# An attention and mixture-of-experts kernel: constants in one transfer, some normalisations on ScalarE, and a new order of all steps

## The chip, the cores and the metric

The kernel runs on one core of a Trainium2 chip. The metric is the device time of one execution in microseconds (us), over several executions. Matrix products run on TensorE (PE in the profile; its weight loads are shown as PEld), the other work on VectorE (DVE), ScalarE (ACT) and GpSimd (POOL); SyncE (SP) issues nearly all DMAs.

## The reference

There are 8 batches, 8 heads, 576 positions and a head width of 64. Head by head and batch by batch an attention is computed whose scores get a bias that depends on the two positions:

```python
scores = q @ k.T / 8
x      = log1p(|i - j|) / log1p(max(i, 1))        # 576 x 576
bias   = relu(x * w1 + b1) @ w2                   # hidden width 32, one bias per head
attn   = softmax(scores + bias);  y = attn @ v
```

The result, as 4608 tokens of width 512, goes through a soft mixture of experts: `logits = y @ phi` (32 slots, four per expert); a softmax over the tokens makes the inputs of the slots, each expert applies two weight matrices (512 x 1024, relu, 1024 x 512), and a softmax over the slots spreads the outputs over the tokens.

## The kernel before

**Units and tiles.** A head pair of one batch is a unit. The first head pair is cut in two halves of the rows (units 0 to 7 and 8 to 15, two tiles of 128 rows each, and half a fifth tile), the other three pairs are units 16 to 39 with four tiles and half a fifth. A tile `p` of unit `u` goes through these steps, and each has a short name:

- `S`: scores of both heads of the pair on PE, into two pairs of PSUM banks (line 517, or line 523 where the tile is done in four quarters; that is what a `+` means here).
- `t`: DVE adds the bias to the scores of one head and finds the row's extreme (line 534). `e`: ACT takes the exponential and the row sum (line 542). `a` and `m`: a small addition (line 549, on POOL, or on DVE with a `+`) and the reciprocal on DVE (line 553).
- `n`: the normalisation, a multiplication of the tile's 576 columns by one number per row, on POOL (lines 436 and 561).
- `T` and `R`: PE transposes the normalised tile into PSUM (line 495); `c` and `cR`: ACT or DVE (`+`) copy that to SBUF (line 439).
- `M0` to `M2`: the product with v on PE (line 629), `x`: its copy to SBUF, `xs`: its store.

**The bias tables.** Before and between the first units, 36 jobs make the bias: `f` (four features of a job, DVE at line 977, or ACT at line 975 with a `+`), `B` (PE, line 987), `E` (ACT at line 997, or DVE with a `+`), `D` (SP writes the result to DRAM, line 1006). `b0` to `b4` read a chunk of 128 rows of it back for a head pair (line 425); chunk 3, for example, needs the jobs 24 to 31.

**The end.** When the last head pair of a batch is done, the steps of the mixture follow (`fx`, `K`, `KR`, `L`, `D`, `d`, `W`, `C`, `Z`; `dq` contains a memset of a small tile on POOL, line 780, for which the transposes of `C` wait). Behind the last unit come the experts (`F`, `H`, `U`, `V`, `s`) and the output (`o`, `p`, `P`). `w` and `r` fetch the 64 tiles of expert weights of 512 KB.

**What sets the order.** Every step is registered with its name, and the string `ORDER` lists all 2644 of them. An entry is `name/unit`, a `+` where there is a choice of the engine (or of the form of `S`), and after `@` the PSUM banks. The program is written out in this order, so each engine and SP's queue get their instructions in the order in which the string has them; every engine works through its own in order. All bulk transfers but one go through SP, and SP, too, waits in order: a transfer that must wait for a buffer or for a write to land holds back all behind it.

**The first transfers.** `tabs` is loaded by ACT's queue, `cols` (w1, b1, w2) and `cons` (a table of reciprocals, and `rowm`) by SP, lines 336 to 338. DVE computes from them `scl` (line 341), which every `f` needs, `nb1` (line 356) and four parts of `wbd` (line 361).

Of the kernel before, what the change touches and what calls it, by code (L numbers as in the profile page):

```python
# [24 lines left out]
wm/-1 f13.2/-1+ f13.0/-1+ f14.2/-1 f9.1/-1 f13.3/-1+ f15.3/-1+ f15.0/-1 f15.1/-1+ f13.1/-1 f14.0/-1 B13/-1@0  # L25
f9.0/-1+ f15.2/-1 f12.0/-1+ f9.3/-1 B15/-1@2 f8.2/-1+ E15/-1 f9.2/-1 B9/-1@4 E9/-1 f11.1/-1+ f14.1/-1
f11.0/-1 f14.3/-1 B14/-1@6 E14/-1 f10.2/-1 f10.3/-1+ f12.1/-1 f12.2/-1 f12.3/-1 B12/-1@2 E12/-1 f11.2/-1
f11.3/-1 f10.1/-1 B11/-1@4 E11/-1 D9/-1 f10.0/-1 B10/-1@6 f23.0/-1+ f8.0/-1 D14/-1 f8.3/-1 f8.1/-1
B8/-1@2 D15/-1 E10/-1 D12/-1 f19.1/-1 f19.3/-1+ E13/-1+ D11/-1 f16.0/-1+ D13/-1 f19.0/-1 f19.2/-1
B19/-1@4 D10/-1 E8/-1+ f21.3/-1 f21.2/-1 D8/-1 f21.1/-1+ f21.0/-1 B21/-1@0 f18.1/-1+ f18.2/-1 f16.2/-1+  # L30
f18.0/-1 f18.3/-1 B18/-1@6 E19/-1 D19/-1 E21/-1 f20.2/-1 D21/-1 f16.1/-1 f16.3/-1 B16/-1@2 b1/-1
f23.1/-1 f23.2/-1 f17.1/-1 f23.3/-1+ B23/-1@4 f17.3/-1 f17.2/-1+ E16/-1+ f20.1/-1 f17.0/-1+ D16/-1 f20.3/-1+
f22.0/-1+ f20.0/-1 B17/-1@0 B20/-1@2 f22.1/-1+ E18/-1+ D18/-1 f22.3/-1+ E17/-1 D17/-1 f3.1/-1+ f22.2/-1
B22/-1@6 E22/-1 E23/-1+ E20/-1+ f0.1/-1 f5.0/-1 f5.3/-1+ f5.2/-1+ f0.2/-1+ f5.1/-1 D23/-1 f0.0/-1+
f0.3/-1 D20/-1 S1/0@0,4 t1.1/0 t1.0/0 e1.0/0 e1.1/0 S1/1+@2,6 t1.1/1 t1.0/1 D22/-1 b2/-1
f3.3/-1 B5/-1@4 f1.0/-1+ f1.1/-1 E5/-1 B0/-1@0 E0/-1 S2/0@6,2 e1.1/1 lq/2 f1.3/-1 e1.0/1
a1/0 m1/0 f1.2/-1 B1/-1@4 f3.0/-1 f3.2/-1 E1/-1 f4.3/-1 D1/-1 B3/-1@0 f2.3/-1 n1.0/0
n1.1/0 T1/0@4 E3/-1 f6.3/-1+ f2.2/-1 a1/1 D3/-1 f2.0/-1 f2.1/-1 c1/0 f4.1/-1 B2/-1@0
E2/-1 f4.0/-1 f4.2/-1 t2.1/0 e2.1/0 t2.0/0 e2.0/0 f6.1/-1+ f27.1/-1+ B4/-1@4 E4/-1+ D2/-1
a2/0+ m2/0 n2.1/0 n2.0/0 S2/1+@2,0 lq/3 m1/1 t2.0/1 e2.0/1 t2.1/1 S1/2+@6,4 t1.1/2  # L40
t1.0/2 e2.1/1 a2/1+ m2/1 T2/0@2 c2/0 f7.1/-1 S2/2@0,4 t2.1/2 t2.0/2 f24.0/-1 R2/0@6
M0/0@2 f7.3/-1 D0/-1 f25.2/-1+ cR2/0 n1.1/1 f24.1/-1+ n1.0/1 T1/1@6 c1/1 n2.1/1 n2.0/1
T2/1@4 R2/1@0 cR2/1+ e2.1/2 f7.2/-1 c2/1+ f7.0/-1 M1/0 e2.0/2 f24.2/-1+ S1/3+@6,0 t1.1/3
M2/0 f26.1/-1 f6.2/-1 x/0 xs/0 M0/1@4 a2/2 m2/2 e1.1/2 B7/-1@2 M1/1 lq/4
t1.0/3 f35.3/-1 e1.1/3 e1.0/2 a1/2+ m1/2 f27.3/-1 lv/2 S2/3+@0,6 f6.0/-1 t2.0/3 f26.0/-1+
E7/-1 M2/1 t2.1/3 D7/-1 f27.0/-1+ f27.2/-1 x/1 xs/1 e1.0/3 n2.1/2 n2.0/2 lv/3
# [1231 lines left out]
```

## Time and profile before

| | |
|---|---|
| three executions | 566.37, 567.01, 569.01 us (median 567.01) |
| the profiled execution | 566.71 us, its span 564.7 us |
| PE, PEld busy | 537.2 us (95%), 358.6 us (64%) |
| DVE, ACT, POOL busy | 430.8 us (76%), 435.8 us (77%), 232.7 us (41%) |
| DMA | 117.15 MB, mean 207 GB/s |

The profile is one execution. The busy time of an engine is the union of its instructions; PE's matmuls are pipelined and their ends are modelled, so PE can look busy where it is slowed down. Where an engine was idle before an instruction, the trace names what released it. The chain of waits is followed back from the last instruction. All times in the rows are counted from the start of the span.

### The profile page before, as it was taken

To read this page: it belongs to the slowest core of one execution; us is meant where nothing else is said; L and a number is where in the kernel's file an instruction comes from. 1 tells how busy PE (TensorE), PEld (TensorE's weight loads), DVE (VectorE), ACT (ScalarE), POOL (GpSimd) and SP (SyncE) were. 2 spreads that over 40 slices of the span, in tenths; PEclk is the share of its full clock that TensorE was granted. 3 is DMA by queue.
4 is the path that set the end of the run, shared out by engine and by line. 5 is a ranking of instruction groups with operands and counts; after the bars stand their busy time and mean duration, and the time that the engine had idled before them with its cause. 6 is when DMAs were issued, how large, how long until landed. Compare 5 with 4: busy or idle time off the path is not lost.

```text
span 564.7 us, 23724 instructions
## 1 busy us (share of the span) xinstructions
PE 537.2 (95%) x9991; PEld 358.6 (64%) x9991; DVE 430.8 (76%) x1188; ACT 435.8 (77%) x922; POOL 232.7 (41%) x365
## 2 busy tenths in 40 slices
PE   8989999999999999999999999999999899999883
PEld 5546665777786667766676666666666566753652
DVE  7999997777888878788876887887889777652241
ACT  7999997898878789887889887887877688641162
POOL 4034434464654545665464655553434354200000
PEclk9999999999999999999999999999999999989998
DMA  6854799667934334194543438455232708989988
GB/s 193 311 179 131 229 293 358 201 182 229 313 107 152 120 116 144 45 345 120 192 165 86 143 130 272 163 202 201 89 107 102 260 6 294 375 294 379 393 342 336
DMA packets 46553, 117.15 MB, mean 207 GB/s; under 512 B 5488, under 2 KB 9712, under 8 KB 46448
## 3 DMA queue, kind: packets, MB, share of 16 engines
q1 hardware_dynamic: 46304, 115.35, 59.2%
q8 instruction: 78, 1.28, 0.9%
q10 hardware_dynamic: 144, 0.29, 0.1%
q14 instruction: 27, 0.22, 0.1%
HBM read 87.01 MB, written 28.62 MB: 205 GB/s over the span
## 4 chain that ended last, share of the span: by engine, by line
PE 72%; DVE 8%; ACT 5%; DMA 3%; issue 3%; POOL 1%; SPq 1%; ACTq 0%; DVEq 0%; POOLq 0%
PE ps L629 22%; PE ps L523 17%; PE ps L495 17%; PE ps L517 5%; DVE y L534 4%; PE ps L1074 2%; ACT y L542 2%; PE ps L1147 2%; DVE f L977 2%; PE ps L709 1%; DMA out_dram<-ob 1%; PE ps L851 1%; DMA qk<-in_qk_dram 1%; DMA bias_m<-e 1%; ACT ob L439 1%
## 5 line engine op out<-in xcount | busy, mean ns | idle before, releaser
L436 POOL TENSOR_SCALAR y<-y,sm 128x576 f32<-128x576 f32 x288 | 212.8, 756 | 158.9 <-DVE sm L553 124.4
L542 ACT ACTIVATE y<-y,mn 128x576 f32<-128x576 f32 x288 | 220.6, 769 | 18.5 <-DVE mn L534 12.5
L534 DVE CUSTOM_DVE_ANT_0 y<-ps,bm 128x576 f32<-128x576 f32 x256 | 184.4, 752 | 39.6 <-PE ps L523 28.5
L629 PE MATMUL ps<-at,v 64*64 64x288 f32 (+2 forms) x2880 | 163.2, 358 | 0.6 <-issue 0.3
L523 PE MATMUL ps<-qk 64*64 64x512 f32 (+1 forms) x1840 | 139.3, 409 | 0.6 <-DVE mn L534 0.3
L439 ACT COPY at<-ps 128x1024 f32<-128x1024 f32 (+2 forms) x125 | 99.7, 806 | 28.1 <-PE ps L495 23.9
L523 PEld LDWEIGHTS ps<-qk 64*64 64x64 f32 x1840 | 78.5, 132 | 66.2 <-issue 47.8
L629 PEld LDWEIGHTS ps<-at,v 64*64 64x64 f32 x2880 | 99.4, 133 | 27.0 <-issue 1.2
L495 PE MATMUL ps<-ident,y 64*128 64x64 f32 x2592 | 105.5, 227 | 5.9 <-DVE mn L534 2.5
L495 PEld LDWEIGHTS ps<-ident,y 64*128 64x128 f32 x2592 | 92.0, 139 | 25.4 <-POOL y L436 10.3
L439 DVE COPY at<-ps 128x1024 f32<-128x1024 f32 (+2 forms) x99 | 85.3, 875 | 7.6 <-PE ps L495 6.7
L542 ACT ACTIVATION_READ_ACCUMULATOR y<-y,mn 128x1 f32 x288 | 54.6, 190 | 0.0
L549 POOL TENSOR_SCALAR sm<-sm 128x2 f32<-128x2 f32 x56 | 12.7, 226 | 86.8 <-ACT y L542 84.5
L977 DVE TENSOR_SCALAR f<-tabs,scl,nb 128x352 f32<-128x352 f32 (+17 forms) x94 | 44.6, 530 | 0.5 <-DMA bias_m<-e 0.4
L987 PE MATMUL ps<-f,wbd 128*32 128x512 f32 (+46 forms) x640 | 41.6, 390 | 2.5 <-DVE f L977 1.7
L517 PE MATMUL ps<-qk 64*128 64x64 f32 (+1 forms) x232 | 37.0, 433 | 0.0
L975 ACT ACTIVATE f<-tabs,cols,scl 128x368 f32<-128x368 f32 (+16 forms) x50 | 34.2, 735 | 2.4 <-DVE scl L341 1.9
L987 PEld LDWEIGHTS ps<-f,wbd 128*32 128x32 f32 x640 | 20.0, 109 | 20.8 <-issue 10.4
L517 PEld LDWEIGHTS ps<-qk 64*128 64x128 f32 x232 | 22.3, 188 | 12.9 <-issue 11.3
L439 ACT COPY xts<-ps 128x576 f32<-128x576 f32 (+2 forms) x32 | 17.3, 541 | 17.0 <-PE ps L629 13.6
L553 DVE RECIPROCAL sm<-sm 128x2 f32<-128x2 f32 x144 | 22.7, 162 | 8.2 <-POOL sm L549 5.6
L534 DVE CUSTOM_DVE_ANT_0 y<-ps,br 128x576 f32<-128x576 f32 x32 | 23.4, 751 | 6.9 <-PE ps L523 5.1
(148 smaller groups left out, 387.7 us busy)
## 6 DMA issues: line engine op xcount, KB each, us to landing
wt<-in_moe_w_dram SPq DMA_DIRECT2D x62, 512.0 KB, 7.0
qk<-in_qk_dram SPq DMA_DIRECT2D x32, 576.0 KB, 4.8
bias_m<-e SPq DMA_DIRECT2D x40, 295.5 KB, 3.8
v<-in_v_dram SPq DMA_DIRECT2D x40, 288.0 KB, 4.1
bm<-bias_m SPq DMA_DIRECT2D x16, 576.0 KB, 5.5
out_dram<-ob SPq DMA_DIRECT2D x16, 512.0 KB, 4.6
xo<-xs SPq DMA_DIRECT2D x8, 864.0 KB, 4.7
xs<-xts SPq DMA_DIRECT2D x16, 288.0 KB, 4.7
```

Source lines behind the costliest of these rows:

```text
L436: nc.gpsimd.tensor_scalar(out=out, in0=y, scalar1=r, scalar2=1.0, op0=ALU.mult, op1=ALU.mult)
L439: (nc.vector.tensor_copy if eng else nc.scalar.copy)(out=out, in_=in_)
L495: nc.tensor.matmul(out, src[rs], ident[rs, rs], is_transpose=True, start=True, stop=True, tile_position=(64 * r, 0))
L517: nc.tensor.matmul(pss[hh].t[:, n, 0:w], x[rs, S + QP[p]:S + QP[p] + P], x[rs, ks], start=True, stop=True, tile_position=(64 * hh, 0))
L523: nc.tensor.matmul(pss[hh].t[64 * r:64 * r + 64, n, 0:w], x[rs, q0:q0 + 64], x[rs, ks], start=True, stop=True, tile_position=(64 * hh, 64 ...
L534: nc.vector.tensor_tensor_reduce(out=d["y", p][:, :, hh], in0=blocks(d["ps", p][hh].read().rearrange("a n j -> a (n j)")[:, 0:S]), in1=blo ...
L542: nc.scalar.activation(out=y, in_=y, func=AF.Exp, bias=d["mn", p][:, hh:hh + 1], scale=-1.0, accum_out=d["sm", p][:, hh:hh + 1])
L553: nc.vector.reciprocal(out=r, in_=r)
L629: nc.tensor.matmul(d["po"].t[64 * c:64 * c + 64, hh, 0:n], d["v"][rs, 64 * k:64 * k + 64], at[0][rs, k, c, cs], start=k == 0, stop=k == 8, ...
L975: nc.scalar.activation(out=f, in_=tabs[:, 0:n], func=AF.Relu, bias=cols[:, 1:2], scale=sc)
L977: nc.vector.tensor_scalar(out=f, in0=tabs[:, 0:n], scalar1=sc, scalar2=nb1[:, 0:1], op0=ALU.mult, op1=ALU.max)
L987: nc.tensor.matmul(pb.t[32 * t:32 * t + 32, a // 512, a % 512:a % 512 + c1 - c0], wbd, x, start=True, stop=True, tile_position=(0, 32 * t))
```

## The change

Three things are changed. First, the constants: one array holds w1, b1, w2, `rowm` and the reciprocals, and one DMA brings it; DVE's computation of `scl` is written ahead of those of `nb1` and `wbd`; `rowm` is copied to a tile of its own by POOL. Second, a `+` at a step `n` puts this normalisation on ACT as a copy with a scale, and 31 of the 288 entries have it: 6 in the units 0 to 10, 21 in the units 13 to 31, 4 in the units 34 to 38. Third, the string `ORDER` is new. It has the same 2644 steps; four pieces of some 80 steps stand at the same places as before (around the units 10 to 12, 24 and 25, 32 and 33, 37 to 39), the pieces between them are rearranged, and the engine of many copies, sums and features is another. Counted in the string, DVE has 12 more large copies and evictions of 512 columns and more than before (`c`, `kc`, `p`, `E`) and 15 fewer of the small sums `a`.

```diff
-    cols = const.tile([P, 2 + H], F32, name="cols")
-    cons = const.tile([P, NJ + 2], F32, name="cons")
+    cons = xp.tile([P, 2 * NJ + H + 4], F32, name="cons", tag="xk")
     nc.scalar.dma_start(out=tabs, in_=tabh)
-    nc.sync.dma_start(out=cols, in_=wcol)
-    nc.sync.dma_start(out=cons, in_=consth)
-    rowm = cons[:, NJ:]
-    scl = xp.tile([P, NJ], F32, name="scl", tag="xk")
-    nc.vector.tensor_scalar(out=scl, in0=cons[:, 0:NJ], scalar1=cols[:, 0:1], scalar2=None, op0=ALU.mult)
+    nc.sync.dma_start(out=cons[:, 0:NJ + H + 4], in_=consth)
+    cols, scl = cons[:, 0:2 + H], cons[:, NJ + H + 4:]
+    rowm = const.tile([P, 2], F32, name="rowm")
+    nc.vector.tensor_scalar(out=scl, in0=cons[:, H + 4:NJ + H + 4], scalar1=cols[:, 0:1], scalar2=None, op0=ALU.mult)
...
+        nc.gpsimd.tensor_copy(out=rowm, in_=cons[:, 2 + H:4 + H])
...
-            def scale(_, g=g):
-                y = d["y", p][:, :, g]
-                norm(y, y, d["sm", p][:, g:g + 1])
+            def scale(eng, g=g):
+                y, r = d["y", p][:, :, g], d["sm", p][:, g:g + 1]
+                if eng:
+                    nc.scalar.activation(out=y, in_=y, func=AF.Copy, scale=r)
+                else:
+                    norm(y, y, r)
...
-n1.1/3 B24/-1@0 R2/3@6 E27/-1 D27/-1 m2/4 cR2/3+ T1/3@4 c1/3+ f29.1/-1 E24/-1 T2/3@2
...
+m1/17 e3.1/17 S1/18+@6,0 a3/17+ t1.0/18 e0.0/17 m3/17 e0.1/17 e1.0/18 t1.1/18 n2.0/17 e1.1/18
```

How three places look on the engines. At the program's start, DVE had this, with `nb_112` for `nb1` and `f` for the features:

```order
L358 MEMSET wbd 128x32
L364 MEMSET stM 128x1
L356 TENSOR_SCALAR nb_112<-cols 128x1
L361 TENSOR_SCALAR wbd<-cols 32x8 x4
L341 TENSOR_SCALAR scl<-cons,cols 128x144
L977 TENSOR_SCALAR f<-tabs,scl,nb_112 128x352
```

and now has this:

```order
L357 MEMSET wbd 128x32
L363 MEMSET stM 128x1
L339 TENSOR_SCALAR cons<-cons 128x144
L355 TENSOR_SCALAR nb_110<-cons 128x1
L360 TENSOR_SCALAR wbd<-cons 32x8 x4
L979 TENSOR_SCALAR f<-tabs,cons,nb_110 128x416
```

The scales stand ahead of the five small instructions; the first feature stays behind all of them.

On SP, where the last jobs of the bias are written out (`bias_m<-e`) and the chunks 0 and 3 are read back (`bm<-bias_m`), before the first tiles of unit 8; the first piece is before, and its last `qk` is that of unit 9:

```order
L425 DMA bm<-bias_m 128x2x576
L1006 DMA bias_m<-e 128x591 x4
L425 DMA bm<-bias_m 128x2x576
L418 DMA v<-in_v_dram 128x576
L413 DMA qk<-in_qk_dram 128x832
L641 DMA xs<-xts 256x1x128 x2
L413 DMA qk<-in_qk_dram 128x1152
L1006 DMA bias_m<-e 128x591 x7
L425 DMA bm<-bias_m 128x2x576
L1006 DMA bias_m<-e 128x591 x4
L413 DMA qk<-in_qk_dram 128x1152
```

and now:

```order
L412 DMA qk<-in_qk_dram 128x832
L643 DMA xs<-xts 256x1x128
L417 DMA v<-in_v_dram 128x576
L412 DMA qk<-in_qk_dram 128x1152
L424 DMA bm<-bias_m 128x2x576
L1008 DMA bias_m<-e 128x591 x11
L424 DMA bm<-bias_m 128x2x576
L412 DMA qk<-in_qk_dram 128x1152
```

The read of chunk 0 has moved behind the `qk` of unit 8 (in the first piece it is the first row), and the read of chunk 3 behind all eleven writes; the `qk` of unit 9 stays the next after that group.

On POOL, around the memset of `lq` of unit 35, where the next normalisations are those of the units 37 and 38 and `sm` is the small addition; first before, then now:

```order
L436 TENSOR_SCALAR y<-y,sm 128x9x64 x10
L549 TENSOR_SCALAR sm<-sm 128x2 x2
L436 TENSOR_SCALAR y<-y,sm 128x9x64 x4
L780 MEMSET lq 128x64
L549 TENSOR_SCALAR sm<-sm 128x2
```

```order
L435 TENSOR_SCALAR y<-y,sm 128x9x64 x6
L548 TENSOR_SCALAR sm<-sm 128x2
L435 TENSOR_SCALAR y<-y,sm 128x9x64 x4
L548 TENSOR_SCALAR sm<-sm 128x2 x2
L782 MEMSET lq 128x64
L435 TENSOR_SCALAR y<-y,sm 128x9x64 x4
```

The memset stood directly behind a normalisation, and now stands behind two small additions.

## Rows read from the trace of the kernel before

**Rows 1.** Busy time of the engines over the whole span, and the engines' shares of the chain of waits (page, parts 1 and 4).

```profile
PE 537.2 (95%) x9991; PEld 358.6 (64%) x9991; DVE 430.8 (76%) x1188; ACT 435.8 (77%) x922; POOL 232.7 (41%) x365
PE 72%; DVE 8%; ACT 5%; DMA 3%; issue 3%; POOL 1%; SPq 1%; ACTq 0%; DVEq 0%; POOLq 0%
```

**Rows 2.** Busy time by stretch: the stretch in us, its length, then PE, PEld, DVE, ACT and POOL (with the count of instructions), PE's granted clock, the share of the DMA engines and GB/s. The four in the middle are four units each.

```profile
6.30:30.00 23.70, 22.67 (x320) 12.20 (x324) 23.19 (x57) 22.86 (x39) 3.87 (x2) 1.00 0.76 265
...
80.00:104.80 24.80, 23.44 (x536) 16.32 (x528) 18.99 (x48) 19.43 (x41) 8.94 (x14) 1.00 0.91 300
...
177.50:227.60 50.10, 49.95 (x880) 33.48 (x879) 40.66 (x116) 42.40 (x92) 26.52 (x41) 1.00 0.36 113
227.60:277.40 49.80, 49.46 (x882) 33.53 (x884) 41.01 (x118) 42.43 (x91) 27.35 (x42) 1.00 0.53 182
277.40:328.00 50.60, 49.51 (x874) 35.48 (x873) 38.95 (x118) 44.18 (x95) 28.15 (x42) 1.00 0.45 146
328.00:378.10 50.10, 49.79 (x873) 32.12 (x870) 40.66 (x112) 40.99 (x90) 26.25 (x42) 1.00 0.57 196
...
537.30:564.70 27.40, 17.07 (x342) 11.68 (x342) 7.24 (x11) 11.75 (x17) 0.00 (x0) 0.95 0.89 346
```

**Rows 3.** The chain of waits between 300 and 330 us: start, length, what. L629 is `M`, L523 `S` in quarters, L517 `S` undivided, L495 the transposes.

```profile
304.53 1.23 PE ps L523 x14
...
310.30 1.46 PE ps L629 x24
311.75 0.97 PE ps L523 x16
```

**Rows 4.** The first microseconds in order of time: start, length, engine and instruction, and in brackets the engine's idle time before it and what ended it; and from the page's list of DMA issues the KB and the median time from issue to landing.

```profile
0.73 0.40 ACTq L336 DMA_DIRECT2D tabs<-in_tab_dram  x1
0.74 0.38 SPq L337 DMA_DIRECT2D cols<-in_wcol_dram  x1
3.44 0.15 DVE L356 TENSOR_SCALAR nb<-cols 128x1 f32<-128x1 f32 x1 [2.53 <-DMA cols<-in_wcol_dram]
3.51 0.68 DVE L361 TENSOR_SCALAR wbd<-cols 32x8 f32<-32x8 f32 x4
4.22 0.29 DVE L341 TENSOR_SCALAR scl<-cons,cols 128x144 f32<-128x144 f32 x1
4.55 4.87 ACT L975 ACTIVATE f<-tabs,cols,scl 128x368 f32<-128x368 f32 x8 [1.89 <-DVE scl L341]
4.55 2.00 DVE L977 TENSOR_SCALAR f<-tabs,scl,nb 128x352 f32<-128x352 f32 x5
...
tabs<-in_tab_dram ACTq DMA_DIRECT2D x1, 288.0 KB, 3.1
cons<-in_const_dram SPq DMA_DIRECT2D x1, 73.0 KB, 2.8
```

**Rows 5.** Groups of instructions by line and shape over the whole span: count, busy us, mean ns of one, idle time before them and what ended it.

```profile
L542 ACT ACTIVATE y<-y,mn 128x576 f32<-128x576 f32 x288 | 220.6, 769 | 18.5 <-DVE mn L534 12.5 <-DVE sm L553 2.5 <-POOL y L436 2.4
L436 POOL TENSOR_SCALAR y<-y,sm 128x576 f32<-128x576 f32 x288 | 212.8, 756 | 158.9 <-DVE sm L553 124.4 <-PE ps L495 7.0 <-ACT e L997 5.1
```

**Rows 6.** Waits of PE and of its weight loads: us in total, times, longest.

```profile
PE ps L495 <- POOL lq L780: 1.7, 1, 1.7
PE ps L495 <- POOL y L436: 1.6, 2, 1.0
...
PEld ps L495 <- POOL y L436: 10.3, 21, 1.1
```

**Rows 7.** SP between 70 and 92 us, and PE around 96 us; at 71.69 chunk 0 is read, at 79.15 the `qk` of unit 8, at 86.58 chunk 3, at 90.39 the `qk` of unit 9. The last three rows are of the page's list of DMA issues.

```profile
71.69 0.47 SPq L425 DMA_DIRECT2D bm<-bias_m  x1
...
79.15 0.56 SPq L413 DMA_DIRECT2D qk<-in_qk_dram  x1
79.80 5.88 SPq L1006 DMA_DIRECT2D bias_m<-e  x7
86.58 0.69 SPq L425 DMA_DIRECT2D bm<-bias_m  x1
87.69 2.60 SPq L1006 DMA_DIRECT2D bias_m<-e  x4
90.39 0.89 SPq L413 DMA_DIRECT2D qk<-in_qk_dram  x1
...
96.25 0.78 PE L495 MATMUL ps<-ident,y 64*128 64x64 f32 x19 [1.02 <-issue]
97.28 2.18 PE L523 MATMUL ps<-qk 64*64 64x512 f32 x32 [0.25 <-DMA qk<-in_qk_dram]
...
bias_m<-e SPq DMA_DIRECT2D x40, 295.5 KB, 3.8
bm<-bias_m SPq DMA_DIRECT2D x16, 576.0 KB, 5.5
```

**Rows 8.** POOL and then PE around 449 us, in order of time.

```profile
448.61 0.75 POOL L436 TENSOR_SCALAR y<-y,sm 128x576 f32<-128x576 f32 x1 [2.44 <-DVE sm L553]
449.30 0.15 POOL L780 MEMSET lq<- 128x64 f32 x1
...
449.51 0.27 PE L495 MATMUL ps<-ident,lq 64*128 64x64 f32 x1 [1.66 <-POOL lq L780]
```

**Rows 9.** PE in the last stage: a wait that no releaser explains.

```profile
533.41 0.63 PE L1147 MATMUL ps<-wt,hT 128*32 128x128 f32 x11 [1.58 <-issue]
```

More of the change, by code (lines that the diff above doesn't have):

```diff
@@ L30 @@
[L30 to L34, printed above, removed]
@@ new lines @@
+T2/7@2 c2/7 e0.0/8 lq/9 t3.1/8 a0/8 e3.1/8 t3.0/8 e3.0/8 S0/9+@0,4 t0.1/9 lv/6
+lv/7 S4/8@6,2 t0.0/9 M0/7@4 m0/8 n0.0/8 b4/-1 t4.1/8 M0/6@0 t4.0/8 a3/8+ xs/4
+m3/8 n3.0/8 n0.1/8 M1/7 M1/6 S3/9+@2,6 t3.1/9 xs/5 e0.1/9 e0.0/9 a0/9+ m0/9
+M2/6 t3.0/9 e4.1/8 e4.0/8 a4/8 m4/8 n0.0/9 n3.1/8+ lq/10 x/6 M2/7 x/7
+R3/8@6 cR3/8 T0/8@0 c0/8+ T3/8@4 S0/10@2,6 t0.1/10 e3.1/9 c3/8 n4.1/8 n4.0/8 R4/8@0
+t0.0/10 n0.1/9+ T4/8@4 cR4/8 c4/8 S3/10+@0,6 lq/11 t3.1/10 e3.0/9 a3/9 m3/9 n3.1/9
+n3.0/9 lv/8 M0/8@2 t3.0/10 M1/8 w1/21 lv/9 e0.0/10 e3.1/10 S4/10@4,6 t4.0/10 M2/8
@@ new lines @@
+T1/39@4 c1/39+ kc01/38 T0/39@2 R1/39@6 fx/39 cR1/39+ D/38@0 C/37@4 c0/39 M0/39@2 M1/39
+d3/37 cC/33 d1/38 d2/38 M2/39 d3/38 cA/37 dq/38 x/39 W/38@6 wc/38 J1/38@1
+J2/38 L/39@4 lc/39 J3/38 wy4/39 Z/38@2 wy3/39 J4/38 J5/38 J6/38 D/39@6 dq/39
+wy1/39 KR/39@4 zc/38 wat/39 d1/39 krc/39 krd/39+ K01/39@2 kc01/39+ K23/39@4 wxt/39 wxo/39
+d2/39 W/39@6 J7/38 F1/38 F2/38@0 kc23/39 wc/39+ Z/39@2 C/39@4 wxk/39 F3/38 zc/39
+Tt/39@0 C/38@6 Tc/39 F0/39@2 wv/39 r0/39 r1/39 r2/39 r3/39 F1/39 r4/39 r5/39
+r6/39 r7/39 F2/39 F3/39 cB/37 cC/37 J8/38 r8/39 r9/39 r10/39 d3/39 cC/34
@@ L1235, in _tables @@
     rowm = np.stack([(sl // 4 == 4 * Q + g[:, 0]) for Q in range(2)], axis=1).astype(np.float32)
-    return {"tab": tab, "const": np.concatenate([invp, rowm], axis=1)}
+    return {"tab": tab}, np.concatenate([rowm, invp], axis=1)
 def _lay(q, k, v):
@@ L1256 @@
     every = dict(zip(("qk", "v"), _lay(inputs["q"], inputs["k"], inputs["v"])))
-    every["wcol"] = np.tile(np.concatenate([inputs["w1"].T, inputs["b1"][:, None], inputs["w2"]], axis=1), (4, 1))
+    wcol = np.tile(np.concatenate([inputs["w1"].T, inputs["b1"][:, None], inputs["w2"]], axis=1), (4, 1))
     every.update({n: inputs[n] for n in ("moe_phi", "moe_w1")})
     every["moe_w2"] = inputs["moe_w2"].reshape(8, 8, 128, 4, 128).transpose(0, 3, 2, 1, 4).reshape(8, 4, 128, 1024)
-    every.update(_tables())
+    tables, const = _tables()
+    every.update(tables)
+    every["const"] = np.concatenate([wcol, const], axis=1)
     for name, a in every.items():
```

423 lines of the change are left out of this document (207 added, 216 removed).

## The prediction, made before the changed kernel was run

> **What bounds the kernel now.** I read the busy shares first, then the chain of waits, then the busy time by stretch, and only then single places. PE is busy for 95% of the span, and 72% of the chain lies on it [rows 1]. The stretches show where. Between 177.5 and 378.1 us four stretches of four units each take 50.1, 49.8, 50.6 and 50.1 us, with 873 to 882 matmuls in each, and PE is busy in all but 0.15, 0.34, 1.09 and 0.31 us [rows 2]. Equal work takes an equal time there, and ACT has at least 6.4 us to spare in each, DVE 8.8: PE sets the pace. The chain shows at what pace: a third of a product with v takes 1.46 us, scores in quarters between two of them 0.97 us, and behind transposes 14 of their 16 instructions 1.23 us [rows 3]. So PE's time there is the work and the number of changes between kinds of work.
>
> Other stages have other limits. From 6.3 to 30 us DVE is busy for 23.19 and ACT for 22.86 of 23.7 us, with the features of the bias; PE is fed by them. From 80 to 104.8 us the DMA engines are busy for 91%, while DVE and ACT stand still for 5.8 and 5.4 us [rows 2]. From 537.3 us on the outputs are written, at 346 GB/s [rows 2].
>
> **The change part by part.** The sum goes against the profiled execution: 566.71 us, of which the span is 564.7 and 2.0 lies around it. It stands 0.3 us below the median of the runs, 567.01.
>
> *The start.* DVE waits for `cols` until 3.44 us, then does `nb` and four parts of `wbd` (0.68 us), then `scl` from 4.22; both ACT and DVE begin with features at 4.55 [rows 4]. The one array takes the place of `cols` in SP's queue, issued at 0.74; with the 2.8 us of `cons` it lands at 3.54, `scl` (0.29 us) is done at 3.83, and `tabs`, 3.1 us behind its issue at 0.73, lands at the same time. ACT can begin at about 3.9, so 0.65 us earlier. DVE still has `nb` and `wbd` ahead of it, and begins at 3.83 + 0.08 + 0.68 = 4.6, as before. Both are full in this stage, and share the work: half of 0.65, **-0.3 us**; the ends are 0 (DVE alone decides) and -0.65. The copy of `rowm` on POOL is hidden behind POOL's idle time, 59% of the span.
>
> *The normalisations.* 31 of them leave POOL, at 756 ns each (23.4 us), and come to ACT. No row shows this form on ACT; the nearest is the exponential of the same tile at 769 ns [rows 5], which makes 23.8 us on an engine that is idle for 129 us. What can it give? A tile's two normalisations need not run one behind the other on POOL any more, so that its transposes could start up to 0.76 us earlier. But PE waited for a normalisation only twice, 1.6 us together; the 10.3 us in 21 waits of its weight loads are hidden behind matmuls that still run [rows 6]. What can it cost? An exponential behind it on ACT comes 0.77 us later, and ACT has 5% of the chain, 28 us of its 436 busy ones [rows 1], one in fifteen: of 23.8 us that is 1.6. I take **0**, with the ends -1.6 and +1.6.
>
> *The new order in the PE-bound units.* I counted the string between the last step of PE of unit 16 and that of unit 32. PE's steps are the same ones. There are 143 changes between kinds of step where there were 141; 32 of the 72 score steps stand between two products where 31 did; 56 instead of 58 are in quarters. At the 0.26 us between 1.23 and 0.97 [rows 3] that is nothing. What is left to gain are PE's waits, 1.9 us in the four stretches [rows 2]; I take a third, **-0.6 us**, with ends -1.9 and +2, since new waits can come as well. DVE's 12 more large copies and evictions, less 15 small sums, lie in the 8.8 us and more that it has free in each of these stretches; if that cover were gone, they would count with their whole length.
>
> *The memset of `lq`.* At 449.51 PE waits 1.66 us for a memset of 0.15 us, which stood on POOL behind a normalisation of 0.75 us, which had waited for DVE's reciprocal [rows 8]. Now two small additions stand there. The 0.75 us goes, and some of the wait ahead of it: **-0.9 us**, between 0 and -1.66.
>
> *The jam at 80 us.* SP issues seven writes of the bias from 79.80 us on, the read of chunk 3 at 86.58, four more writes, and the `qk` of unit 9 at 90.39; this lands 6.75 us later, and PE loses 1.02 and 0.25 us around it [rows 7]. In the new queue the read of chunk 3 is behind all eleven writes, and that of chunk 0 is in the same crowd instead of at 71.69. The best case is that all 1.3 us goes. The worst is rival B. I take **-0.4 us**, since the writes' sources are placed a little earlier in the string.
>
> *The end.* PE's 1.58 us at 533.41 has no releaser [rows 9], so nothing in the order takes it away, nor the outputs' time: **0**, with ends of -1.6 and +1.6.
>
> The sum is -0.3 + 0 - 0.6 - 0.9 - 0.4 + 0 = -2.2 us, and 566.7 - 2.2 = **564.5 us**.
>
> **The rivals.** *A: the waits go almost everywhere.* Then PE isn't at its pace, and the chain's 28% off PE is room. For it speaks the jam: without it the 5.8 us of DVE are worth some 3 us, and 0.65 at the start, 1.9 in the middle, 1.66 at the memset come to it: 566.7 - 7.2 = 559.5 us. Against it speaks that equal units take 50 us four times. The Trainium skill (Perfetto Trace Analysis, section Identifying the Most-Contended Engine) says that the busy time of matmuls is a bad measure of the distance to the limit and the share of weight loads a better one; that share is 64% here, so by the rule A is likelier than by my reading. The trace agrees in part: the stretches before 105 us have such room, the four equal ones show none.
>
> *B, slower: the read of chunk 3 comes too late.* The place is SP's queue at 80 to 95 us. Four more writes ahead of it, at the 2.60 us that four took, and chunk 0's 576 KB at the stretch's 300 GB/s, 2.0 us, shift it and the `qk` behind it by 4.6 us [rows 2, 7]. The chunk needs 5.5 us to land; DVE takes its tiles in order, and all later tiles wait behind those of unit 8. PE is the bound from there on, so the 4.6 us stay to the end: with the -0.3 of the start, and the rest of the gains used up by delays of the next units, 566.7 - 0.3 + 4.6 = 571 us. If the `lq` and middle gains stay, 569.5. It decides if the read of chunk 3 is issued after about 88 us. Against it: the last jobs stand earlier in the string than before.
>
> *C, slower: ACT becomes the bound.* From 277.5 to 328 it is busy for 44.18 of 50.6 us [rows 2]; five or six normalisations of 0.77 make 48.4. If half of the 20 in the units 16 to 31 hold up PE by their whole length, 7.7 us: 572 us with the other terms.
>
> *D: the waits come back at other places*, and only the start stays: 566.4 us.
>
> **How the numbers follow.** The forecast has 0.55; its own range is 562 to 567. A has 0.17, B 0.13, C 0.05, D 0.10. A measurement of this kernel can tell about 0.5% from no change, 2.8 us: faster is below 564.2, slower above 569.8. The forecast lies near the first bound, so a little less than half of it is faster, 0.26, and with A 0.43; slower is C and most of B, 0.16; 0.41 is left for the same. The range reaches down to A and up to B: 559 to 570.5; below it lies half of A, above it half of B and C, under 0.2.
>
> **What would show it.** The start is right if ACT's first feature begins near 3.9 us. The middle is right if four units still take 49.5 to 50.5 us; if they take 48 or less, A is right and my reading of PE's pace wrong. The memset is right if PE's wait for `lq` is under 1 us. Rival B shows as a DVE wait on `bm` or a PE wait on `qk` of some us near 90 to 100 us; C as PE waits whose releaser is ACT's line of the normalisation. If the 31 instructions take far more than 0.77 us each, the second term is wrong.

## The result: 0.8% slower, and the profile after

Six executions of the changed kernel took 571.05 to 574.2 us, median 572.72; six of the kernel before on the same chip 566.37 to 569.01, median 568.18. The ratio is 1.0083, with a 95% interval of 1.0058 to 1.0108. The prediction, 564.5 us with a range of 559 to 570.5, had the wrong sign, and the time is outside its range.

The profiled execution of the changed kernel has a span of 571.4 us, against 564.7. I first looked for where the 6.7 us arise. The step `x` of each unit (the copies `xts<-ps`, counted in the order of the string) can be found in both traces; the table gives the start of some of them, of the experts' first product, of the first output and the end, in us.

| | before | after | difference |
|---|---|---|---|
| `x` of unit 0 | 49.0 | 54.7 | +5.8 |
| `x` of unit 5 | 94.0 | 98.9 | +4.9 |
| `x` of unit 8 | 113.8 | 120.1 | +6.3 |
| `x` of unit 16 | 177.5 | 183.9 | +6.4 |
| `x` of unit 32 | 378.1 | 384.5 | +6.4 |
| `x` of unit 35 | 428.4 | 434.7 | +6.3 |
| `x` of unit 37 | 466.6 | 470.3 | +3.7 |
| `x` of unit 39 | 494.6 | 498.5 | +3.9 |
| first product of the experts | 508.0 | 511.2 | +3.2 |
| first output issued | 537.3 | 542.8 | +5.5 |
| end of the span | 564.7 | 571.4 | +6.7 |

Most is lost before unit 0 is done, the 16 units in the middle neither win nor lose, the units 35 to 37 win 2.6 us, and the end loses 2.8 again. PE's granted clock is 1.00 in both traces from 20 to 503 us, so between these times the differences aren't the clock's.

The page's busy times and chain [rows 1], after:

```profile
PE 540.6 (95%) x9951; PEld 359.5 (63%) x9951; DVE 435.0 (76%) x1178; ACT 448.3 (78%) x948; POOL 211.5 (37%) x350
PE 76%; DVE 9%; ACT 6%; DMA 4%; issue 2%; POOL 1%; ACTq 0%; DVEq 0%; POOLq 0%
```

They show the change (ACT 12.5 us more, POOL 21.2 less), and nothing of the loss: PE is as busy as before in its share. Neither do the four stretches of [rows 2], in the same columns; they are at the same times, so what is done in them now lies 6.4 us earlier in the program:

```profile
177.50:227.60 50.10, 49.46 (x864) 32.18 (x856) 40.10 (x114) 44.14 (x94) 25.37 (x41) 1.00 0.34 111
227.60:277.40 49.80, 49.27 (x890) 32.50 (x892) 39.47 (x110) 45.04 (x96) 24.06 (x39) 1.00 0.50 167
277.40:328.00 50.60, 49.51 (x856) 36.55 (x852) 40.58 (x120) 46.21 (x99) 24.59 (x37) 1.00 0.47 150
328.00:378.10 50.10, 49.72 (x880) 33.03 (x876) 41.91 (x113) 42.95 (x94) 24.71 (x40) 1.00 0.54 186
```

From the `x` of unit 16 to that of unit 32 both kernels take 200.6 us.

**The start.** In order of time, after, as in [rows 4]:

```profile
3.93 0.87 DVE L339 TENSOR_SCALAR cons<-cons 128x144 f32<-128x144 f32 x1 [3.02 <-DMA cons<-in_const_dram]
3.96 0.19 POOL L345 COPY rowm<-cons 128x2 f32<-128x2 f32 x1 [2.12 <-DMA cons<-in_const_dram]
4.08 0.63 POOL L351 MEMSET et<- 128x640 f32 x1
...
4.83 5.52 ACT L977 ACTIVATE f<-tabs,cons 128x432 f32<-128x432 f32 x9 [2.17 <-DVE nb L355]
5.45 2.12 DVE L979 TENSOR_SCALAR f<-tabs,cons,nb 128x416 f32<-128x416 f32 x5
```

The scales take 0.87 us where they took 0.29, and the first features are 0.3 us (ACT) and 0.9 us (DVE) later than before. The larger loss comes at 12 us, where after has these rows (the first is DVE's, the second PE's, then two of SP):

```profile
15.12 0.88 DVE L979 TENSOR_SCALAR f<-tabs,cons,nb 128x384 f32<-128x384 f32 x2 [3.00 <-DMA bias_m<-e]
15.66 6.86 PE L989 MATMUL ps<-f,wbd 128*32 128x208 f32 x74 [3.10 <-DVE f L979]
11.02 0.34 SPq L1008 DMA_DIRECT2D bias_m<-e  x1
16.78 9.07 SPq L1008 DMA_DIRECT2D bias_m<-e  x9
```

and before had these:

```profile
14.19 0.52 DVE L977 TENSOR_SCALAR f<-tabs,scl,nb 128x320 f32<-128x320 f32 x1 [0.38 <-DMA bias_m<-e]
10.73 2.84 SPq L1006 DMA_DIRECT2D bias_m<-e  x4
```

DVE stands still for 3.00 us until a write of the bias has landed. The feature is `f12.0`; it was given the buffer of job 11, the first that is written out. SP issued that write at 11.02, and it landed 4.0 us later. Behind DVE's feature is the eviction `E13` (of job 13, at 15.92), and SP's second write, `D13`, waits for that until 16.78; the other writes stand behind it. PE runs dry from 12.56 to 15.66 us. Before, the first feature in a written-out buffer was due in DVE's queue at 13.81 us for 12.12 and waited 0.38 us, and SP had issued four writes by 13.57.

The stop has a second effect. By stretch, with the columns of [rows 2]:

```profile
12.00:13.00 1.00, 0.56 (x9) 0.12 (x2) 0.13 (x1) 1.00 (x3) 0.00 (x0) 1.00 0.70 253
13.00:14.00 1.00, 0.00 (x0) 0.00 (x0) 0.00 (x0) 1.00 (x3) 0.00 (x0) 1.00 0.04 7
...
17.00:18.00 1.00, 1.00 (x13) 0.48 (x8) 1.00 (x4) 0.84 (x2) 0.00 (x0) 0.50 0.39 147
...
20.00:21.00 1.00, 1.00 (x21) 0.68 (x13) 1.00 (x4) 0.44 (x1) 0.00 (x0) 1.00 0.11 45
```

Behind PE's pause its granted clock is 0.50 (1.2 GHz) from 16.4 to about 20 us: 13 matmuls begin in the microsecond from 17 us, and 21 in that from 20 us, at 1.00.

**The jam at 80 us.** SP, DVE and PE, after; at 84.11 chunk 0 is read, at 97.00 chunk 3, at 97.47 is the `qk` of unit 9 [rows 7]:

```profile
84.11 0.39 SPq L424 DMA_DIRECT2D bm<-bias_m  x1
86.12 8.47 SPq L1008 DMA_DIRECT2D bias_m<-e  x11
97.00 0.37 SPq L424 DMA_DIRECT2D bm<-bias_m  x1
97.47 0.64 SPq L412 DMA_DIRECT2D qk<-in_qk_dram  x1
102.30 0.76 DVE L533 CUSTOM_DVE_ANT_0 y<-ps,bm 128x576 f32<-128x576 f32 x1 [1.58 <-DMA bm<-bias_m]
103.73 2.18 PE L522 MATMUL ps<-qk 64*64 64x512 f32 x32 [1.29 <-DMA qk<-in_qk_dram]
```

Between the steps `x` of the units 5 and 8 another 1.4 us are lost here; by unit 12 the difference is 5.9 again. It is a reading of one trace: with the same order at this place, e8 below loses 1.4 us there too, and e13 nothing (2.8 us behind at unit 5, 2.6 at unit 8).

**The end.** The chain of waits from the experts' first product on, before and then after:

```profile
507.98 8.83 PE ps L1074 x78
...
531.83 1.58 issue
...
545.32 3.45 DMA out_dram<-ob
...
552.18 3.65 DMA out_dram<-ob
```

```profile
511.23 10.50 PE ps L1076 x80
...
534.38 1.70 issue
...
544.66 4.75 DMA out_dram<-ob
...
555.33 4.61 DMA out_dram<-ob
```

The first 80 of the experts' 128 products (78 before) take 1.7 us more; PE's granted clock is 0.50 from 508.0 to 514.8 us in this execution, and was from 503.8 to 507.2 before, ahead of these products. The wait that no releaser explains [rows 9] is still there, 1.70 us. In the outputs both chains have two writes that an output buffer waits for; they are 3.45 and 3.65 us before and 4.75 and 4.61 after, 2.3 us more together.

### The profile page after: what moved, and what is told of

Same layout as the page of the kernel before. It is cut to its first block, busy times and chain, and to the rows that moved or that the text cites. A ratio compares the mean times of both kernels' runs of the same rounds, so it can differ in the third digit from the quotient of the medians.

```text
span 571.4 us, 23635 instructions
## 1 busy us (share of the span) xinstructions
PE 540.6 (95%) x9951; PEld 359.5 (63%) x9951; DVE 435.0 (76%) x1178; ACT 448.3 (78%) x948; POOL 211.5 (37%) x350
## 4 chain that ended last, share of the span: by engine, by line
PE 76%; DVE 9%; ACT 6%; DMA 4%; issue 2%; POOL 1%; ACTq 0%; DVEq 0%; POOLq 0%
PE ps L631 23%; PE ps L522 17%; PE ps L494 16%; PE ps L516 5%; PE ps L989 4%; DVE f L979 3%; DVE y L533 3%; PE ps L1076 3%; ACT y L541 2%; DVE at L438 2%; PE ps L1149 2%; DMA out_dram<-ob 2%; PE ps L711 2%; PE ps L853 1%; DMA qk<-in_qk_dram 1%
## 5 line engine op out<-in xcount | busy, mean ns | idle before, releaser
L435 POOL TENSOR_SCALAR y<-y,sm 128x576 f32<-128x576 f32 x257 | 190.1, 754 | 147.2 <-DVE sm L552 98.1
L522 PE MATMUL ps<-qk 64*64 64x64 f32 (+1 forms) x1760 | 133.5, 409 | 2.0 <-DMA qk<-in_qk_dram 1.3
L631 PEld LDWEIGHTS ps<-at,v 64*64 64x64 f32 x2880 | 99.8, 133 | 28.4 <-issue 1.8
L522 PEld LDWEIGHTS ps<-qk 64*64 64x64 f32 x1760 | 75.4, 132 | 66.3 <-issue 46.4
L438 DVE COPY at<-ps 128x1024 f32<-128x1024 f32 (+2 forms) x99 | 88.4, 902 | 12.0 <-PE ps L494 10.6
L548 POOL TENSOR_SCALAR sm<-sm 128x2 f32<-128x2 f32 x71 | 16.1, 227 | 125.9 <-ACT y L541 124.0
L989 PE MATMUL ps<-f,wbd 128*32 128x79 f32 (+49 forms) x640 | 42.8, 403 | 6.8 <-DVE f L979 6.1
L979 DVE TENSOR_SCALAR f<-tabs,cons,nb 128x448 f32<-128x448 f32 (+17 forms) x95 | 45.0, 533 | 3.1 <-DMA bias_m<-e 3.0
L516 PE MATMUL ps<-qk 64*128 64x64 f32 (+1 forms) x272 | 44.2, 434 | 0.1
L516 PEld LDWEIGHTS ps<-qk 64*128 64x128 f32 x272 | 27.7, 188 | 14.2 <-issue 13.2
L977 ACT ACTIVATE f<-tabs,cons 128x384 f32<-128x384 f32 (+17 forms) x49 | 34.3, 752 | 2.7 <-DVE nb L355 2.2
L438 ACT COPY xts<-ps 128x576 f32<-128x576 f32 (+2 forms) x33 | 17.6, 535 | 11.1 <-PE ps L631 10.0
```

Of the source, the lines that this page charges most:

```text
L435: nc.gpsimd.tensor_scalar(out=out, in0=y, scalar1=r, scalar2=1.0, op0=ALU.mult, op1=ALU.mult)
L438: (nc.vector.tensor_copy if eng else nc.scalar.copy)(out=out, in_=in_)
L516: nc.tensor.matmul(pss[hh].t[:, n, 0:w], x[rs, S + QP[p]:S + QP[p] + P], x[rs, ks], start=True, stop=True, tile_position=(64 * hh, 0))
L522: nc.tensor.matmul(pss[hh].t[64 * r:64 * r + 64, n, 0:w], x[rs, q0:q0 + 64], x[rs, ks], start=True, stop=True, tile_position=(64 * hh, 64 ...
L631: nc.tensor.matmul(d["po"].t[64 * c:64 * c + 64, hh, 0:n], d["v"][rs, 64 * k:64 * k + 64], at[0][rs, k, c, cs], start=k == 0, stop=k == 8, ...
L977: nc.scalar.activation(out=f, in_=tabs[:, 0:n], func=AF.Relu, bias=cols[:, 1:2], scale=sc)
```

## Experiments

The new string can be taken apart. At each of the four pieces that stand at the same places in both strings the same steps have been done, so a kernel can have the old order up to such a piece and the new one behind it; the PSUM banks are renamed where the two meet, nothing else. All kernels here have the constants as changed. Their line numbers are 64 lower than those of the changed kernel (PE's transposes are line 430 for 494, the normalisations 371 on POOL and 497 on ACT). Ratios are to the kernel before on the same chip; a difference of two ratios is uncertain by 0.25 to 0.4%, some 2 us, where nothing else is said.

**e1: the start in the old order.**

```diff
-f10.1/-1 f9.0/-1+ f11.3/-1+ f11.1/-1+ f13.3/-1+ f15.1/-1+ f11.2/-1 f12.1/-1+ wm/-1 f10.3/-1+ f9.2/-1
+wm/-1 f13.2/-1+ f13.0/-1+ f14.2/-1 f9.1/-1 f13.3/-1+ f15.3/-1+ f15.0/-1 f15.1/-1+ f13.1/-1 f14.0/-1
...
```

> The changed kernel with the first part of the order of before, up to the product of unit 12 (the constants in one transfer and the scales first stay, and so do the 25 ACT normalisations behind that point). Between the two traces the step x of unit 10 starts 6.6 us later in the changed kernel, and no unit after it adds to that. Theory 'the loss is in the order of the start': the start of the scores comes back by some 5.5 us, and the time is 572.7 - 6.3 = 566.4 us (565 to 568). Rival 'the constants': the scale instruction of 0.87 us and the later first features stay, so most of the loss stays: 571 to 573. Rival 'the end takes it back': the last weights bind the end, so that a gain ahead of them is lost: 569.5 to 571.

Median 568.0 us, ratio 1.0012 (0.9993 to 1.0032). Against the changed kernel's 1.0083 the start is worth 0.7%, 4.0 us. In the trace `x` of unit 0 is 1.3 us behind the kernel before, where it was 5.8. So most of the loss lies in the order of the start, and the constants don't carry it. But 568.0 is at the upper edge of the first expectation's range: of the 6.3 us that it hoped for, 4.0 came. Some was lost anew: 2.1 us between the units 12 and 13 (1.6 by unit 16), behind a bias chunk that SP reads at 142.70:

```profile
142.70 0.39 SPq L360 DMA_DIRECT2D bm<-bias_m  x1
150.88 0.76 DVE L469 CUSTOM_DVE_ANT_0 y<-ps,bm 128x576 f32<-128x576 f32 x1 [1.47 <-DMA bm<-bias_m]
151.79 0.34 PE L430 MATMUL ps<-ident,y 64*128 64x64 f32 x4 [1.31 <-DVE sm L484]
```

DVE is released 8.2 us after the issue of this read, and 7.2 us in the changed kernel, where it waits only 0.21 us.

**e2: the end in the old order.** The string of before from the mixture of unit 37 on, all else as changed.

> The changed kernel with the last part of the order of before, behind the first bias job of unit 37's mixture; all else as changed. From the last step x to the end of the span the changed kernel takes 72.9 us and the kernel before 70.1. Theory 'the end of the new order costs 2.8 us by itself': 572.7 - 2.8 = 569.9 us (569 to 571). Rival 'the end is late only because the start was': 572.2 to 573.2.

570.43 us, ratio 1.0048 (1.0022 to 1.0075): by itself the end of the new order costs 0.35%, 2.0 us. The interval overlaps that of the changed kernel (1.0058 to 1.0108), so this run alone doesn't show it; e12 and e13 below support it.

**e3: the constants alone**, in the old order.

> The kernel before with the constants in one transfer and the scales first alone; order and engines as before. Theory 'the order of the start': the first features of DVE begin some 0.9 us later, as in the changed kernel's trace (5.45 for 4.55), ACT's 0.3 us later, and the time is 568.2 + 0.3 to 0.9 = 568.8 us (568 to 569.5). Rival 'the constants': 572 us or more. The prediction's own term: 568.2 - 0.3 = 567.9.

567.61 us, ratio 0.9999 (0.9985 to 1.0013), a little under the first expectation's range; the rival, 572 us or more, falls. In the trace `x` of unit 0 is 1.2 us late and that of unit 16 0.6; in the time nothing is left that can be measured.

**e4: all normalisations on POOL, in the new order.**

```diff
-n2.1/1+
+n2.1/1
...
-n3.0/38+
+n3.0/38
```

> The changed kernel with all 288 normalisations on POOL; the order is the changed one otherwise. Theory 'they cost and give nothing': 572.7 us, within 0.8. Rival 'ACT holds up PE': 570.5 us or less. Rival 'they are what makes the units 34 to 38 2.6 us shorter': 574.5 us or more.

584.93 us, ratio 1.0293 (1.027 to 1.0316): 12 us slower than the changed kernel. Only the number of the third expectation holds, and not its reason: the loss is made between the units 13 and 30 (at `x` of unit 32 this kernel is 13.4 us behind the changed one, at unit 10 1.4). Part of it comes with PE's clock, which in this trace falls to 0.50 for 3.4 us each at 99, 154 and 191 us. PE's waits, by line: total us, times, longest:

```profile
PE ps L430 <- POOL y L371: 12.5, 19, 2.3
```

So the 31 instructions on ACT save 12 us in the new order. Is it a gain of theirs, then?

**e7: the same 31 on ACT, in the old order.**

> The order of before with the constants as changed and the same 31 normalisations on ACT, each where it stood on POOL. In the changed order they are worth 12 us (584.9 us without them, PE waiting 12.5 us for POOL's normalisations). Theory 'they only mend what the new order breaks': in the old order, where PE waited 1.6 us for POOL, they give nothing and cost a little on ACT: 567.5 to 569. Rival 'they are a gain by themselves': 565.5 us or less. Rival 'ACT holds up PE': 570 us or more.

589.63 us, ratio 1.039 (1.0361 to 1.0419): 22 us slower. The theory (567.5 to 569) fails by far, and the rival 'ACT holds up PE' has the number. PE's waits for normalisations, which were 1.6 us for POOL before [rows 6], are now for both engines, and one place of them:

```profile
PE ps L430 <- ACT y L497: 6.8, 6, 1.5
PE ps L430 <- POOL y L371: 5.5, 5, 1.8
...
240.14 1.35 PE L430 MATMUL ps<-ident,y 64*128 64x64 f32 x36 [1.47 <-POOL y L371]
242.72 0.72 PE L430 MATMUL ps<-ident,y 64*128 64x64 f32 x16 [1.24 <-ACT y L497]
```

They are 10.7 us more than they were, for both engines; the rest of the 22 us I have not traced wait by wait (PE's clock falls three times for 3.4 us in this trace too). So the second and the third part of the change can't be priced alone: against the kernel before, the new order without the 31 costs 2.9% (e4), the 31 without the new order 3.9%, and both together 0.8%; in the traces both together cost nothing from unit 16 to unit 32.

**e5 and e6: old start and end, or all old but the units 34 to 38.**

> The order of before in the start (to the product of unit 12) and in the end (from the mixture of unit 37), the changed order between, constants as changed; 21 of the normalisations that lie between the two cuts are on ACT, and those of the units 34 to 38 there. Theory 'start and end carry the loss, the units 34 to 38 a gain, and the parts add up': the start gave 4.7 us back and the end 2.3, so 572.7 - 7.0 = 565.7 us (564.5 to 567). Rival 'the parts don't add up, since the last weights and the outputs bind the end': 567.5 to 569.

566.17 us, ratio 0.9991 (0.9964 to 1.0018). It is inside the expected range, but not measurably faster than before: the wait for the bias chunk of e1 is in it as well (1.04 us), and `x` of unit 13 is 1.7 us later against before than that of unit 12.

> The order of before everywhere but between unit 33 and the mixture of unit 37, where the changed order stands with its ACT normalisations; constants as changed. In the traces the units 33 to 38 take 2.2 us less in the changed kernel (6.0 us behind at unit 33, 3.8 at unit 38). Theory 'that gain is real and stays to the end': 567.5 - 2.2 = 565.3 us (564.5 to 566.3). Rival 'the end is bound by the transfers of the last weights and outputs, and takes it back': 567 to 568.

563.95 us, ratio 0.9945 (0.9924 to 0.9966), 0.55% faster than before, and under the expected range. The gain of the units 34 to 38 is real, about 3 us (2.2 were expected), and is not taken back at the end.

**e8: two features exchanged in the new order.**

```diff
-f16.0/-1+ f14.3/-1 f12.2/-1 f10.2/-1 f12.0/-1
+f12.0/-1 f14.3/-1 f12.2/-1 f10.2/-1 f16.0/-1+
```

> The changed kernel with two entries of its order exchanged: the feature f12.0 of DVE and the feature f16.0 of ACT. The buffer of the first job that is written out (job 11) then goes to ACT's feature and not to DVE's; nothing else moves on any engine. Theory 'DVE's 3.0 us wait for the first write to land is the seed of the loss at the start': the wait leaves DVE, the second write is issued near 14 us for 16.8, PE's stop from 12.6 to 15.7 us goes, and the time is 572.7 - 3.0 = 569.7 us (568.5 to 570.5). Rival 'the loss is spread over the whole start, and the queue of writes behind D13 sets it': less than 1 us, 571.7 to 573.

568.92 us, ratio 1.0040 (1.0019 to 1.0061): 3.8 us less by the medians, 2.4 by the ratios. DVE and SP at the same place as above:

```profile
12.67 0.82 DVE L933 TENSOR_SCALAR e<-ps,bcon 128x591 f32<-128x591 f32 x1
10.86 11.09 SPq L944 DMA_DIRECT2D bias_m<-e  x10
```

DVE's wait is gone, the eviction `E13` runs at 12.67 for 15.92, ten writes are issued in 11.1 us where they took 14.8, and PE's clock stays at 1.00 here. The wait for the first write has passed to ACT, where it is 1.06 us (`f16.0`, at 14.93). `x` of unit 5 is as early as before (94.0), where it was 4.9 us late. Two entries of 2644, with no instruction more or less, are most of the loss of the start (2.4 of 4.0 us by the ratios). What stays is the jam: `x` of unit 8 is 1.5 us late.

**e13: both repairs**, the exchange of e8 and the end of e2.

> The changed kernel with both repairs: the two features exchanged as in e8, and the order of before from the mixture of unit 37 on as in e2. Theory 'two separate causes': 3.8 us from the first and 2.3 from the second, so 572.7 - 6.1 = 566.6 us (565.3 to 567.6). Rival 'they overlap, since the last weights and the outputs bind the end': 568.0 to 569.0.

567.41 us, ratio 0.9999 (0.9971 to 1.0027), inside the first range: the two add up, and with them the changed kernel is as fast as the one before. It isn't faster, although it has the gain of the units 34 to 38; against e6 (0.9945) some 3 us are still lost, in the trace ahead of them (`x` of unit 32 is 3.3 us behind), and these two repairs don't touch those.

**e9: POOL's copy of `rowm` later**, in the kernel of e6.

```diff
-        nc.gpsimd.tensor_copy(out=rowm, in_=cons[:, 2 + H:4 + H])
...
         for t in (lp, et, et2):
             nc.gpsimd.memset(t, 0.0)
+        nc.gpsimd.tensor_copy(out=rowm, in_=cons[:, 2 + H:4 + H])
```

> The kernel of e6 with POOL's copy of the row masks moved behind its other work of the start, so that POOL does nothing while DVE makes the scales. In all kernels with the constants as changed the scale instruction took 0.87 us, beside that copy (0.18 us) and then a memset of POOL; before it took 0.29 us with POOL idle. Theory 'DVE's scale instruction is slow because POOL works beside it': 0.3 us, the first features 0.5 us earlier, and 564.0 - 0.5 = 563.5 us. Rival 'it is slow by itself, since its input and output lie in one tile': 0.87 us again, and 564.0.

```profile
3.90 0.29 DVE L275 TENSOR_SCALAR cons<-cons 128x144 f32<-128x144 f32 x1 [3.00 <-DMA cons<-in_const_dram]
...
4.24 1.86 ACT L913 ACTIVATE f<-tabs,cons 128x368 f32<-128x368 f32 x3 [1.58 <-DVE cons L275]
4.89 1.24 DVE L915 TENSOR_SCALAR f<-tabs,cons,nb 128x352 f32<-128x352 f32 x3
```

The scales take 0.29 us when POOL does nothing beside them. The median is 563.48 us, ratio 0.993 (0.9906 to 0.9954), not to be told from e6; and `x` of unit 0 is no earlier than in e6 (50.7 for 49.9), though all features begin 0.6 us earlier. So the moment of the first feature doesn't set this stage.

**e10: the four normalisations of the units 34, 35 and 38 on POOL**, in the kernel of e6.

> The kernel of e6 with its four normalisations of the units 34, 35 and 38 back on POOL. Theory 'the gain there is the memset of lq and the order': within 0.6 us of e6, 564.0. Rival 'the four normalisations on ACT carry it, as all 31 do in the changed order (12 us, 0.4 us each)': 565.5 us or more, with PE waiting for POOL's normalisations between 410 and 480 us.

563.43 us, ratio 0.9927 (0.9898 to 0.9956): the four have no part in the gain there that could be measured.

**e11: the memset of `lq` on DVE**, in the old order.

```diff
-            nc.gpsimd.memset(lq[:, 192:256], 0.0)
+            nc.vector.memset(lq[:, 192:256], 0.0)
```

> The order of before with the constants as changed and one further edit: the memset of lq is on DVE and not on POOL. Theory 'PE's wait of 1.66 us near 450 us is the queue of POOL': the wait goes and 1.0 to 1.7 us stay gained to the end: 567.5 - 1.4 = 566.1 us. Rival 'the end takes it back': 567 to 567.8.

```profile
451.14 0.27 PE L430 MATMUL ps<-ident,lq 64*128 64x64 f32 x1 [0.70 <-DVE lq L718]
```

PE's wait [rows 8] falls from 1.66 to 0.70 us, since the memset now stands in DVE's queue; 566.98 us, ratio 0.9992 (0.9972 to 1.0012), lies between the two expectations and is too little to measure. The new order does it better: it has the memset on POOL at 433.65 us, nobody waits for it, and `x` of unit 37 gains 2.6 us. Of these, 1.66 are this wait. What the other 0.9 are I haven't shown; no single wait of PE answers to them.

**e12: the outputs in the new order**, in the kernel of e6.

> The kernel of e6 with the outputs in the changed order: all steps from the first of the output products on, with the gathering of the second column group moved ahead of them. From the first output's issue to the end the kernels with the end of before took 27.3 to 30.1 us, those with the changed end 28.6 to 30.4. Theory 'the changed end loses in its outputs': 564.0 + 2.0 = 566 us (565 to 567). Rival 'it loses ahead of the outputs, in the experts' first products': 564.0 within 0.6.

565.89 us, ratio 0.9974 (0.9953 to 0.9995), against e6's 0.9945: 0.3%, 1.6 us, of the 2.0 that the end costs. e9 and e10 have e6's outputs and ran on the same chip as e12; against their 563.48 and 563.43 us it is 2.4 us, and their executions (562.1 to 565.2) hardly overlap those of e12 (564.1 to 567.8). So the order of the outputs costs time. SP at the first outputs, in e6 and then in e12:

```profile
532.49 5.41 SPq L1125 DMA_DIRECT2D out_dram<-ob  x5
538.53 0.33 SPq L1140 DMA_DIRECT2D out_dram<-ob  x1
```

```profile
536.76 7.55 SPq L1125 DMA_DIRECT2D out_dram<-ob  x6
545.00 0.33 SPq L1140 DMA_DIRECT2D out_dram<-ob  x1
```

The old order has six outputs issued within 6.4 us, the new one within 7.6; from the first to the end of the span it is 27.3 us in e6 and 28.6 in e12. The traces alone wouldn't show it: over all of them this stretch has 27.3 to 30.2 us with the old outputs and 28.6 to 30.4 with the new.

## Why the prediction was wrong, by its own steps

*The start, -0.3 us.* This is the step that failed: the runs showed +5.8 us at unit 0, and +4.0 us of the time (e1), of which e8's exchange of two features takes away 2.4 to 3.8. I had priced it by the moment at which the first feature begins, and had read "both are full in this stage" as a reason why nothing else could go wrong. The order of the 36 jobs was new as well, and I didn't follow it: which buffer each feature gets, when the first written-out buffer is needed again, and what stands behind it on DVE and in SP's queue. [Rows 7] had 3.8 us from issue to landing for such a write, and the trace of before had a wait of 0.38 us of just this kind at 14.19. Its bound, 0 to -0.65, left no room for a loss. The sentence that ACT begins near 3.9 us fell too (4.83), since the array released DVE at 3.93 where 3.54 was expected, and the scales took three times their 0.29 us; by e3 and e9 that matters little.

*The normalisations, 0 (±1.6).* The length was right, and so was that PE hardly waits: in the changed kernel the 31 take 768 ns each (0.77 expected), ACT waits 0.6 us for their reciprocals, and PE 0.3 us for them. Their row, beside that of the exponential [rows 5]:

```profile
L541 ACT ACTIVATE y<-y,mn 128x576 f32<-128x576 f32 x288 | 220.5, 769 | 13.9 <-DVE mn L533 11.6 <-DVE sm L548 1.1 <-POOL sm L548 0.4
L561 ACT ACTIVATE y<-y,sm 128x576 f32<-128x576 f32 x31 | 23.7, 768 | 0.6 <-DVE sm L552 0.6
```

The reason was wrong: I took ACT's 129 idle us for cover, and priced the edit apart from the order. e7 shows that the same edit without the new order costs 22 us, about the whole length of the 31 instructions, and e4 that the changed kernel without it is 12 us slower. That the two come to nothing together in the middle units was not foreseen; the 0 was luck. Rival C's price (7.7 us, for a stretch that begins at 277.4 us in [rows 2] and not at 277.5) was nearer to what the edit does alone than my bounds of ±1.6.

*The middle, -0.6.* Measured 0.0 us from unit 16 to 32. The reading that PE sets the pace there is right (50.4, 49.5, 50.5 and 50.1 us from `x` to `x` for four units each), and rival A with its 559.5 falls. The Trainium skill (Perfetto Trace Analysis, section Identifying the Most-Contended Engine) would judge the room by the share of weight loads, beside that of the peak arithmetic: the first is 64% over the span [rows 1] and 64 to 70% in these stretches [rows 2], and neither the order nor the normalisations moved there won anything.

*The memset of `lq`, -0.9.* Right, and too small: the whole 1.66 us went, and the stretch won 2.6.

*The jam, -0.4.* Wrong sign in the trace: 1.4 us are lost between the units 5 and 8. Rival B named the mechanism and both marks (DVE on `bm` 1.58 us, PE on `qk` 1.29). Its condition was met, since chunk 3 was read at 97.00 and so behind 88 us, but its price of 4.6 was three times too large.

*The end, 0 (±1.6).* e2 gives 2.0 us for it, and e12 shows 1.6 to 2.4 for the order of the outputs alone. The unexplained wait was read rightly (1.58 before, 1.70 after: this order doesn't take it away). That nothing in the order changes the outputs' time was wrong; I hadn't looked at the order in which the outputs become ready.

In sum, by the ratios: start +4.0 us (e1), end +2.0 (e2), units 34 to 38 -3.1 (e6 against e3), which makes 2.9 where 4.7 were measured. e5 against e6 puts another 2.6 us on the units 12 to 33 in the new order, with the wait for the bias chunk behind unit 12. In the changed kernel this wait is 0.21 us, and its late start alone doesn't explain that: in e8, whose `x` of unit 12 is 0.9 us behind the kernel before (e5's 1.1), it is 0.32 us, with the chunk released 7.0 us after its issue and 7.8 in e5. Why the read takes longer behind the old start is not shown, and what of the 2.6 us the changed kernel has stays open. So does the part of PE's clock: the mean granted clock over the executions is 0.988 for the changed kernel and 0.989 to 0.991 for e1, e8 and e12, which have the new outputs, and 0.993 to 0.995 for e2, e3, e5, e6, e9 to e11 and e13, which have the old ones.

## What to carry to other kernels

When an order is replaced, follow the first place where a buffer that a DMA still reads is given out again: the instruction that gets it stops its whole engine until the transfer has landed, and everything behind it in the issuing queue stops with it. Idle time of an in-order engine is by itself no cover for an instruction put between others; the same edit saved 12 us in the order made for it and cost 22 us in the other. Compare traces by the same step of each unit before looking at shares: here the shares were equal, and a table of eleven rows showed that most of the loss was made in the first 50 us.

## What the runs showed of the hardware

**The bytes of a write have moved well before the engine that waits for it is released.** The first write of 295 KB moved its bytes up to about 13 us (the DMA share is 0.70 from 12 to 13 us and 0.04 from 13 to 14), and DVE, which waited for its buffer, started at 15.12. The Trainium skill (DMA: Bandwidth & Descriptors, section Anatomy of one DMA — SWDGE (gpsimd) path) puts about 2 us of a transfer's fixed cost mostly on the receipt of the write; it says so of another kind of queue, and this row, some 2 us, agrees.

**POOL's work can make an instruction of DVE three times as long.** One instruction of DVE took 0.87 us beside two short ones of POOL and 0.29 without them (e9). It ended at 4.80, just behind POOL's memset, which ended at 4.71, although its row begins 0.03 us ahead of POOL's first; POOL's memset took its usual 0.63 us. The Trainium skill (SBUF — State Buffer, section Terms) says that the two engines share a pair of ports and that the loser waits for the whole instruction; the rows agree.

**The clock falls at different places in runs of the same code.** Where PE starves between the last unit and the experts, the granted clock was 0.50 for 3.4 us in the profiled executions of before, e3, e8, e9, e10 and e12 and for 6.8 us in that of after, and stayed at 1.00 there in e1, e2, e4 to e7, e11 and e13. From `x` of unit 39 to the end of the experts' first products e6 took 27.9 us and e9, with the same order, 29.6. The same fall stands elsewhere in some profiles (30.2 to 33.6 us in e13, 99.8 to 103.2 in e11). A difference of 2 us between two single profiles is therefore no evidence where their clocks differ; of the end I trust the medians alone.
